# Two layers of 128x128 products on one core: each product given as two halves of 64 columns

## The chip, the cores and the metric

The kernel runs on one core of one Trainium2 chip. The metric is the device time of one execution in microseconds (us). Engines are named as the profile names them: PE is TensorE's matmuls, PEld its weight loads, DVE is VectorE, ACT is ScalarE, POOL is GpSimd, SP is SyncE, which issues DMAs.

## What is computed

The reference is an attention with a threshold, followed by a feed-forward layer with a squared ReLU, all in float32:

```
scores = scale * np.matmul(q, k.transpose(0, 1, 3, 2))       # q, k, v: (8, 8, 576, 64)
thresh = np.max(scores, axis=-1, keepdims=True) - tau
scores = np.where(scores >= thresh, scores, -1000000000.0)
attn = softmax(scores)
x = (attn @ v).transpose(0, 2, 1, 3).reshape(4608, 512)
h = np.maximum(x @ w_in, 0.0)                                # w_in:  (512, 2048)
out = h * h @ w_out                                          # w_out: (2048, 512)
```

The change touches the last two lines only: the two layers, x by w_in and h * h by w_out.

## The kernel before, in words

The kernel has three parts in order of time. **Attention** comes first: scores (L458), their softmax on DVE and ACT, transposes of the weights (L402, L422), spread sums (L541) and the product with v (L558). The array of TensorE is used there in tiles: L458, L541 and L558 have 64 rows and 64 columns, and the transposes 64 rows and 128 columns. A run of L558 (`values`) goes over nine blocks of keys c, two column halves u and two row halves j, so that its neighbouring calls lie on four different tiles of the array; the two u of one j share the rows and write to the same PSUM bank, into its lower and upper 64 partitions.

**The hidden layer** (`hidden_layer`, from 493.6 to 883 us) goes over 9 steps of 512 tokens each. Both layers multiply blocks by a scheme with 7 products in place of 8, applied twice, an outer index m and an inner index k of seven each, so a step has 49 block products. Sums and differences of the blocks are made on DVE, ACT and POOL before and after the products. The steps are run in passes (L1278 to L1279): step 0 alone, then steps 1 to 6 in pairs, each pair twice with one half h of the output columns, then steps 7 and 8 alone. A block product of a single step is four calls j on L984, each with 128x128 weights and 128 columns of x. A product of a pair of steps is two calls on L977, each with 128x128 weights and 256 columns.

**The output layer** (`output_layer`, from 883 us to the end) goes over the 9 steps, with 49 block products each. A product is four calls on L1119 which add up in PSUM: weights g[:, j, :] (the squared hidden values, 128x128), and 128 columns of w_out.

The order of a block row is written out in `inner` (L759): seven products with k = 1, 6, 7, 5, 2, 4, 3, each followed by its copy (L794, ACT) or sum (L125, DVE) out of PSUM, and by a `tick`, which issues other work: loads and sums for what comes next (`also`, L1295 and L1329), and the ReLU and square of finished tiles (`square`, L944). Products 1, 6, 7 and 5 begin new banks (X, Y, Z, W); products 2, 4 and 3 add to X, Z and W after the first sum has been read from them. Six banks are used in turn. Work on each engine is in program order. Weights stay in the tile `wall`: the 49 blocks of w_in first, which are replaced by those of w_out (L1207) in the last hidden step and at the start of the output layer.

[...] All matmuls are float32, for which the trace has two records of a call (two passes, each with its own weight load); a transpose has one.

Of the kernel before, what the change touches and what calls it, by code (L numbers as in the profile page):

```python
# [48 lines left out]
def kernel(  # L49
# [25 lines left out]
    nc = tc.nc  # L75
    B, H, S, D = q.shape
    P = 128
# [46 lines left out]
    def plus(e, out, x, y):  # L124
        e.tensor_tensor(out=out, in0=x, in1=y, op=ALU.add)  # L125
# [12 lines left out]
    W_IN, W_OUT = {}, {}  # L138
# [146 lines left out]
    HALF = P // 2  # L285
# [226 lines left out]
    for g in range(2, 2 * len(pairs)):  # L512
        two, x = divmod(g - 4, 4)
# [279 lines left out]
    def copy(to, from_):  # L793
        nc.scalar.copy(to, from_)  # L794

    NQ = STEP // 4


# [4 lines left out]
    def load_x(n, parts=XPARTS, slot=None):  # L803
        at = X_AT[n % 2]
        xo = arena[:, ds(at, 7 * BANK)].rearrange("p (m c t) -> p m c t", m=7, c=2)
        for a, c in parts:
            to = xo[:, AT_B[a][c] - 1, :, :] if slot is None else slot

            t0 = n * STEP + c * 2 * NQ
            done = 0  # L810
            while done < 2 * NQ:
                b, at = divmod(t0 + done, S)
                m = min(S - at, 2 * NQ - done)
                src = xT[b][ds(a * 2 * P, 2 * P), ds(at, m)].rearrange("(c p) n -> p c n", p=P)
# [21 lines left out]
    def prepare_x(n, add):  # L836
# [3 lines left out]
        for op, o, x, y in SUMS_B:  # L840
# [5 lines left out]
        of = {  # L846
            1: xo[:, :, 0, 0:NQ], 7: xo[:, :, 0, NQ : 2 * NQ], 2: xo[:, :, 1, 0:NQ], 3: xo[:, :, 1, NQ : 2 * NQ],
            5: xi[:, 0, :, :], 6: xi[:, 1, :, :], 4: xi[:, 2, :, :],
# [14 lines left out]
    def part_x(steps, k, m, count=None):  # L863

        of = slice((steps[0] + 1) % 2, (steps[0] + 1) % 2 + len(steps))
        ms = slice(m - 1, m - 1 + count) if count else m - 1
        if k in (1, 7, 2, 3):
            return places_x[:, of, ms, k in (2, 3), k in (7, 3), :]
        return sums_x[:, of, (5, 6, 4).index(k), ms, :]

    def slot_x(n, m):

        at = X_AT[n % 2]
        if m is None:
            return arena[:, ds(at + 7 * BANK, 3 * 7 * P)].rearrange("p (k z) -> p k z", k=3)[:, 0:2, 0:NQ * 2]
        return arena[:, ds(at + (m - 1) * BANK, BANK)].rearrange("p (c t) -> p c t", c=2)
# [64 lines left out]
    def hidden_bank():  # L941
        return banks.tile([P, BANK], FP32, tag="b", bufs=6, name="ph")
# [15 lines left out]
    def squares_due(wait):  # L958

        if squares and squares[0][0] + wait <= clock["n"]:  # L960
            square(*squares.popleft()[1:])

    def hidden_layer(n, also):

        steps, h = n
        of = prepared.pop(steps[0], None)
        tile4 = lambda tag, bufs: hid.tile([P, 4, NQ], FP32, tag=tag, bufs=bufs)
        bank = lambda: hidden_bank()[:, :].rearrange("p (k t) -> p k t", k=4)
        temp = lambda name: tile4("t", 6)
        U2, U3 = {}, {}  # L970

        for m in OUTER:

            def product(to, k, more):
                if h is not None:
                    for j in range(2):
                        nc.tensor.matmul(  # L977
                            to[:, 2 * j : 2 * j + 2, :], W_IN[m, k][:, ts(2 * h + j, P)], part_x(steps, k, m),
                            start=(not more and j == 0), stop=True, skip_group_check=True,
                        )  # L980
                    return
                x = of[k][:, m - 1, :] if of else part_x(steps, k, m)[:, 0, :]
                for j in range(4):
                    nc.tensor.matmul(  # L984
                        to[:, j, :], W_IN[m, k][:, ts(j, P)], x, start=(not more and j == 0), stop=True,
                        skip_group_check=True,
                    )

            def add(to, c, other, more, t=None):

                if other is None:
                    plus(nc.vector, to, c, more)
                else:
                    plus(nc.gpsimd, to, t, more)

            def final(ab, c, other):
                if m == 1:
                    U2[ab] = tile4("u", 12)
                    if other is None:
                        nc.scalar.copy(U2[ab], c)  # L1000
                    else:
                        plus(nc.vector, U2[ab], c, other)
                    return
                t = None
                if other is not None:
                    t = temp("t")
                    plus(nc.vector, t, c, other)
                if m == 6:
                    add(U2[ab], c, other, U2[ab], t)
                elif m == 7:  # L1010
                    U3[ab] = tile4("u", 12)
                    add(U3[ab], c, other, U2[ab], t)
                else:
                    o = tile4("o", 8)
                    add(o, c, other, U3[ab] if m in (4, 5) else U2[ab], t)
                    if m == 5:
                        add(U2[ab], c, other, U2[ab], t)
                    row, col = {2: (0, 0), 4: (1, 0), 5: (1, 1), 3: (0, 1)}[m]
                    squares.append((clock["n"] + LATER.get(m, 0), n, 4 * (2 * row + ab[0]) + 2 * col + ab[1], o))

            def tick(at):
                clock["n"] += 1
                also(m, at)
                squares_due(6)

            inner(product, copy, temp, bank, final, tick)


# [61 lines left out]
    def output_layer(n, also):  # L1090
        bank = lambda: banks.tile([P, BANK], FP32, tag="b", bufs=6, name="po")[:, 0:P]
        temp = lambda name: fin.tile([P, P], FP32, tag="t")
        AT = {(0, 0): 0, (1, 1): 1, (1, 0): 2, (0, 1): 3}
        U2 = fin.tile([P, 4, P], FP32, tag="u")
        U3 = fin.tile([P, 4, P], FP32, tag="u")
        o = {}

        def give_out(row, ab, queue):

            a, b = ab  # L1100
            to = out[ds(n * STEP + row * 2 * NQ + a * NQ, NQ), :].rearrange("p (c b o) -> p c b o", c=2, b=2)
            if queue is None:
                later.append((to[:, :, b, :], o[row][:, :, AT[ab], :]))
            else:
                queue.dma_start(out=to[:, :, b, :], in_=o[row][:, :, AT[ab], :])

        for m in OUTER:
            where = {2: (0, 0), 4: (1, 0), 5: (1, 1), 3: (0, 1)}.get(m)
            if where and where[0] not in o:
                o[where[0]] = fin.tile([P, 2, 4, P], FP32, tag="o")  # L1110
            mine = U3 if m in (4, 5) else U2
            t3 = fin.tile([P, 3, P], FP32, tag="t3") if m != 1 else None

            at_end = n == NSTEP - 1 and m == OUTER[-1]

            def product(to, k, more):
                g, w = operands[n, m, k], W_OUT[m, k].rearrange("p (k o) -> p k o", k=4)
                for j in range(4):
                    nc.tensor.matmul(  # L1119
                        to, g[:, j, :], w[:, j, :], start=(not more and j == 0), stop=(j == 3), skip_group_check=True  # L1120
                    )

            def sums_to(i, e, c):

                if where:
                    plus(e, o[where[0]][:, where[1], i, :], c, mine[:, i, :])
                if m in (5, 6):
                    plus(e, U2[:, i, :], c, U2[:, i, :])
                if m == 7:
                    plus(e, U3[:, i, :], c, U2[:, i, :])  # L1130

            def final(ab, c, other):
                i = AT[ab]
                if m == 1 and other is None:
                    nc.scalar.copy(U2[:, i, :], c)
                elif m == 1:
                    plus(nc.vector, U2[:, i, :], c, other)
                elif other is None:
                    sums_to(i, nc.vector, c)
                else:  # L1140
                    plus(nc.vector, t3[:, i - 1, :], c, other)
                    if at_end:
                        sums_to(i, nc.vector, t3[:, i - 1, :])
                if at_end:
                    give_out(0, ab, nc.sync if i % 2 else nc.scalar)

            inner(product, copy, temp, bank, final, lambda at: also(m, at))
            if m != 1 and not at_end:
                sums_to(slice(1, 4), nc.gpsimd, t3[:, :, :])
            if m in (5, 3) and not at_end:  # L1150
                for ab in AT:
                    give_out(where[0], ab, None)
# [8 lines left out]
    with tc.manual_schedule():  # L1161
# [149 lines left out]
        for n in range(NSTEP):  # L1311
            more = n + 1 < NSTEP
# [74 lines left out]
```

## Time and profile before

| what | value |
|---|---|
| median of 3 runs | 1287.91 us (1287.0 to 1290.93) |
| the profiled execution | 1285.38 us, of which the span of its instructions is 1283.3 us |
| attention | 0 to about 493 us |
| hidden layer, step 0 (L984) | from 493.6 us |
| hidden layer, steps 1 to 6 (L977) | from 537.4 us |
| hidden layer, steps 7 and 8 (L984) | about 795 to 883.4 us |
| output layer (L1119) | from 883.4 us; its last matmul starts at 1279.4 us |
| mean granted clock of TensorE | 0.996 |

How to read the lines: a group of instructions is given as source line, engine, operation, output<-inputs, the part of the array for TensorE (rows*columns), the shape of the moving data (or of the weights, for a load) and xcount; then the time in which at least one of them ran, the mean length of one in ns, and after the second bar the idle time of the engine before them and what ended it. Lengths of matmuls overlap their neighbours', so that they say little of the rate; counts in a stretch of time do. An answer for a window A:B counts each record that is in flight in it at any moment.

### The profile page before, as it was taken

The page shows a single profiled execution, that of the slowest core. Times are in us where ns is not written, and L with a number is a line of the kernel's source. Part 1 is how long each engine was busy: PE and PEld are TensorE (multiplying, and loading weights), DVE is VectorE, ACT ScalarE, POOL GpSimd, SP SyncE. Part 2 cuts the span into 40 slices and gives each one's busy share as a digit, 9 for nine tenths or more (in the row PEclk, how much of TensorE's full clock was granted, in tenths as well). Part 3 has the DMA queues.
Part 4 walks back from the last instruction along what each step waited for, and adds up shares of the span by engine and source line. Part 5 has one row for each costly group of instructions (what it writes and reads, how often), then busy time and mean ns, then how long its engine had stood idle before and what let it go on. Part 6 is the DMA issues. An engine that isn't in the chain of part 4 may idle for free.

```text
span 1283.3 us, 45875 instructions
## 1 busy us (share of the span) xinstructions
PE 1261.6 (98%) x18287; PEld 1105.9 (86%) x18287; DVE 989.2 (77%) x2384; ACT 846.2 (66%) x1537; POOL 981.5 (76%) x1070
## 2 busy tenths in 40 slices
PE   8999999999999999999999999999999999999998
PEld 5777777777777778988888888999999999999998
DVE  6999999999999994886877878867745664665463
ACT  6999999999999993665766766666423431343240
POOL 2999999777776543987997989758777867786775
PEclk8999999999999999999999999999999999999999
DMA  7566676444333314658767868499544314532411
GB/s 185 141 171 159 170 194 179 115 96 106 91 81 88 95 35 110 200 159 231 214 179 217 228 191 235 149 333 387 182 134 165 116 61 155 165 98 73 160 34 34
DMA packets 291413, 196.20 MB, mean 153 GB/s; under 512 B 100096, under 2 KB 252160, under 8 KB 291200
## 3 DMA queue, kind: packets, MB, share of 16 engines
q1 hardware_dynamic: 289888, 192.87, 51.7%
q8 instruction: 144, 2.36, 0.8%
q14 instruction: 69, 0.57, 0.1%
q10 hardware_dynamic: 1312, 0.41, 0.1%
HBM read 120.85 MB, written 72.35 MB: 151 GB/s over the span
## 4 chain that ended last, share of the span: by engine, by line
PE 75%; DMA 2%; ACT 2%; DVE 1%; issue 1%; SPq 0%; POOL 0%; DVEq 0%; ACTq 0%; POOLq 0%
PE po L1119 29%; PE ph L977 17%; PE ph L984 9%; PE sc L558 7%; PE sc L458 6%; PE pt L402 4%; PE sc L541 1%; PE sc L422 1%; DMA wall<-w 1%; DMA g<-arena 1%; DVE arena L125 1%; ACT arena L946 1%; ACT arena L947 1%; ACT c L833 0%; DMA arena<-xT 0%
## 5 line engine op out<-in xcount | busy, mean ns | idle before, releaser
L125 POOL TENSOR_TENSOR arena<-arena 128x512 f32<-128x512 f32 (+1 forms) x314 | 378.1, 1222 | 135.1 <-DVE arena L125 117.2
L1119 PE MATMUL po<-wall,arena 128*128 128x128 f32 x3528 | 394.8, 275 | 1.4 <-ACT arena L794 1.4
L1119 PEld LDWEIGHTS po<-wall,arena 128*128 128x128 f32 x3528 | 394.3, 192 | 1.8 <-ACT arena L794 1.8
L125 DVE TENSOR_TENSOR arena<-ph,arena 128x512 f32<-128x512 f32 x378 | 255.2, 689 | 78.8 <-PE ph L977 30.3
L122 POOL TENSOR_TENSOR arena<-arena 128x128 f32<-128x128 f32 (+1 forms) x322 | 265.3, 825 | 26.1 <-DMA arena<-w 10.3
L977 PE MATMUL ph<-arena,wall 128*128 128x256 f32 x1176 | 256.3, 380 | 2.1 <-DVE arena L125 1.7
L977 PEld LDWEIGHTS ph<-arena,wall 128*128 128x128 f32 x1176 | 222.1, 190 | 35.9 <-DVE arena L125 6.0
L125 DVE TENSOR_TENSOR arena<-po,arena 128x128 f32<-128x128 f32 x378 | 108.3, 290 | 167.8 <-PE po L1119 163.7
L491 DVE SCALAR_TENSOR_TENSOR arena<-arena 128x576 f32<-128x576 f32 x288 | 226.1, 821 | 0.6 <-ACT arena L486 0.6
L486 ACT ACTIVATE arena<-arena 128x576 f32<-128x576 f32 x288 | 213.8, 780 | 13.1 <-DVE arena L476 13.1
L833 ACT COPY c<-arena 128x512 f32<-128x512 f32 (+1 forms) x295 | 169.1, 579 | 72.7 <-DVE arena L122 35.7
L476 DVE TENSOR_SCALAR_CACHE_REDUCE arena<-sc 128x576 f32<-128x576 f32 x288 | 203.3, 753 | 13.8 <-issue 5.2
L458 PE MATMUL sc<-arena 64*64 64x512 f32 (+1 forms) x2304 | 178.1, 413 | 5.8 <-ACT arena L549 1.7
L558 PE MATMUL sc<-arena 64*64 64x128 f32 (+1 forms) x5760 | 166.0, 262 | 0.8 <-ACT arena L549 0.7
L122 DVE TENSOR_TENSOR arena<-arena,c 128x512 f32<-128x512 f32 x235 | 154.4, 666 | 11.9 <-ACT c L833 8.9
L558 PEld LDWEIGHTS sc<-arena 64*64 64x64 f32 x5760 | 151.3, 134 | 3.9 <-ACT arena L549 0.9
L549 ACT COPY arena<-pt 128x1024 f32<-128x1024 f32 x144 | 145.9, 1013 | 4.3 <-PE pt L402 3.7
L794 ACT COPY arena<-po 128x128 f32<-128x128 f32 x63 | 16.7, 265 | 186.4 <-PE po L1119 183.6
L458 PEld LDWEIGHTS sc<-arena 64*64 64x64 f32 x2304 | 76.4, 134 | 70.7 <-issue 45.7
L984 PE MATMUL ph<-arena,wall 128*128 128x128 f32 x1176 | 132.0, 275 | 0.6 <-DVE arena L691 0.6
L984 PEld LDWEIGHTS ph<-arena,wall 128*128 128x128 f32 x1176 | 131.6, 192 | 0.9 <-issue 0.7
L483 POOL TENSOR_SCALAR arena<-arena,tau_p 128x2 f32<-128x2 f32 x144 | 83.3, 579 | 54.0 <-DVE arena L476 41.0
(54 smaller groups left out, 1142.2 us busy)
## 6 DMA issues: line engine op xcount, KB each, us to landing
arena<-g SPq DMA_DIRECT2D x144, 256.0 KB, 4.8
g<-arena SPq DMA_DIRECT2D x192, 128.0 KB, 2.8
w<-arena SPq DMA_DIRECT2D x60, 256.0 KB, 3.1
wall<-w SPq DMA_DIRECT2D x49, 256.0 KB, 5.2
g<-arena SPq DMA_DIRECT2D x48, 256.0 KB, 3.6
arena<-w SPq DMA_DIRECT2D x44, 256.0 KB, 3.2
arena<-in_v_dram SPq DMA_DIRECT2D x32, 288.0 KB, 3.9
out_dram<-arena SPq DMA_DIRECT2D x70, 128.0 KB, 2.2
```

The costliest lines, as they stand in the source:

```text
L122: e.tensor_tensor(out=out, in0=x, in1=y, op=ALU.subtract)
L125: e.tensor_tensor(out=out, in0=x, in1=y, op=ALU.add)
L458: made = nc.tensor.matmul(sc[at, ds(to, count)], lhs, kT[rows, ds(at_k, count)], start=True, stop=True)
L476: made = nc.vector.tensor_scalar(out=s[:, j, :], in0=sc[:, ds(at, S)], scalar1=1.0, scalar2=None, op0=ALU.mult, op1=ALU.min, accum_out=nmx ...
L486: nc.scalar.activation(out=w[:, :, j, :], in_=of(j), func=AF.Exp, bias=nmx[:, j : j + 1], scale=-1.0)
L491: nc.vector.scalar_tensor_tensor(out=w[:, :, j, :], in0=of(j), scalar=thr[:, j : j + 1], in1=w[:, :, j, :], op0=ALU.is_le, op1=ALU.mult, a ...
L549: touch("weights", nc.scalar.copy(joined(to), whole(pt, 0, count)), at, 2 * BANK, m)
L558: made = nc.tensor.matmul(sc[ds(u * D, D), ds(5 * j * BANK + row, count)], loaded_v[i][rows, (c - (u != j)) % CH, :], wT[m][rows, ds(weigh ...
L833: nc.scalar.copy(c, y)
L977: nc.tensor.matmul(to[:, 2 * j : 2 * j + 2, :], W_IN[m, k][:, ts(2 * h + j, P)], part_x(steps, k, m), start=(not more and j == 0), stop=Tr ...
L984: nc.tensor.matmul(to[:, j, :], W_IN[m, k][:, ts(j, P)], x, start=(not more and j == 0), stop=True, skip_group_check=True,)
L1119: nc.tensor.matmul(to, g[:, j, :], w[:, j, :], start=(not more and j == 0), stop=(j == 3), skip_group_check=True)
```

## The change

A helper `by_tiles` takes the place of `nc.tensor.matmul` at two places. It gives one product as two matmuls: the left 64 columns of the weights into partitions 0 to 63 of the output, then the right 64 columns into partitions 64 to 127. Both have all 128 rows, and both read the same moving data. HALF is 64. The calls with 256 columns (L977) stay as they are.

```
+    def by_tiles(to, lhs, rhs, start, stop):
+
+        for cols in (ds(0, HALF), ds(HALF, HALF)):
+            nc.tensor.matmul(to[cols], lhs[:, cols], rhs, start=start, stop=stop, skip_group_check=True)
...
                 for j in range(4):
-                    nc.tensor.matmul(
-                        to[:, j, :], W_IN[m, k][:, ts(j, P)], x, start=(not more and j == 0), stop=True,
-                        skip_group_check=True,
-                    )
+                    by_tiles(to[:, j, :], W_IN[m, k][:, ts(j, P)], x, not more and j == 0, True)
...
                 for j in range(4):
-                    nc.tensor.matmul(
-                        to, g[:, j, :], w[:, j, :], start=(not more and j == 0), stop=(j == 3), skip_group_check=True
-                    )
+                    by_tiles(to, g[:, j, :], w[:, j, :], not more and j == 0, j == 3)
```

## The prediction

> **What bounds the kernel now.** I read the page's first two parts, then the groups by line with the shapes kept apart, then the stages in windows. The page:
>
> ```profile
> span 1283.3 us, 45875 instructions
> PE 1261.6 (98%) x18287; PEld 1105.9 (86%) x18287; DVE 989.2 (77%) x2384; ACT 846.2 (66%) x1537; POOL 981.5 (76%) x1070
> ...
> PEclk8999999999999999999999999999999999999999
> ...
> PE 75%; DMA 2%; ACT 2%; DVE 1%; issue 1%; SPq 0%; POOL 0%; DVEq 0%; ACTq 0%; POOLq 0%
> ```
>
> TensorE is busy nearly throughout at the full granted clock, and it heads the chain that ended last. Busy alone does not say what a matmul waits for, since matmuls are pipelined; the spacing of their starts does. The groups, matmuls (PE) and their weight loads (PEld):
>
> ```profile
> L1119 PE MATMUL po<-wall,arena 128*128 128x128 f32 x3528 | 394.8, 275 | 1.4 <-ACT arena L794 1.4
> L977 PE MATMUL ph<-arena,wall 128*128 128x256 f32 x1176 | 256.3, 380 | 2.1 <-DVE arena L125 1.7
> L558 PE MATMUL sc<-arena 64*64 64x128 f32 x4608 | 164.0, 273 | 0.8 <-ACT arena L549 0.7
> L984 PE MATMUL ph<-arena,wall 128*128 128x128 f32 x1176 | 132.0, 275 | 0.6 <-DVE arena L691 0.6
> ```
>
> ```profile
> L1119 PEld LDWEIGHTS po<-wall,arena 128*128 128x128 f32 x3528 | 394.3, 192 | 1.8 <-ACT arena L794 1.8
> L558 PEld LDWEIGHTS sc<-arena 64*64 64x64 f32 x5760 | 151.3, 134 | 3.9 <-ACT arena L549 0.9 <-DVE arena L476 0.3
> L402 PEld LDWEIGHTS pt<-ident,arena 64*128 64x128 f32 x2304 | 83.7, 140 | 42.4 <-ACT arena L549 32.7 <-issue 4.6 <-ACT arena L427 1.1
> ```
>
> The code makes 9 x 49 x 4 = 1764 calls on L1119, and the trace has 3528 records: each call is two passes, and each pass loads its own weights. L984 likewise (3 steps, 588 calls, 1176 records). The change touches these two groups and not L977, whose calls have 256 columns. Three windows without a stall, one inside each group (columns: PE, PEld, DVE, ACT, POOL with record counts, clock, DMA share, GB/s):
>
> ```profile
> 640.00:680.00 40.00, 40.00 (x187) 35.20 (x187) 30.61 (x49) 24.98 (x46) 34.89 (x44) 1.00 0.67 183
> 1000.00:1040.00 40.00, 40.00 (x361) 40.00 (x360) 23.59 (x61) 14.21 (x29) 30.89 (x27) 1.00 0.43 133
> 810.00:850.00 40.00, 40.00 (x361) 40.00 (x360) 29.74 (x48) 25.77 (x48) 27.70 (x28) 1.00 0.57 193
> ```
>
> A window counts every record that touches it, so the spacing is (window + length of one record) / count. L1119 (1000:1040) and L984 (810:850): (40.00 + 0.275) / 361 = 111.57 ns a pass. L977 (640:680): (40.00 + 0.379) / 187 = 215.9 ns for 256 columns, so 107.9 ns per 128. So streaming alone does not account for 111.57 ns. The loads do: with 256 columns PEld has gaps (35.20 of 40), with 128 columns it is busy all 40.00. I read L1119 and L984 as **bound by the weight load**, by some 2 to 4 ns a pass, with the stream close behind.
>
> **What the change does to one pass.** It takes away 1764 + 588 calls of 128 x 128 weights and gives twice as many with 64 columns of weights: 4704 passes become 4704 pairs of passes, a left and a right half, each streaming the same 128 columns. All hangs on whether the two halves of a pair run side by side. Before has no tile of 128 rows x 64 columns; the nearest are the 64 x 64 tiles of L558, four on the array, two side by side on the same rows. Two answers in the middle of one run of them, the first for 302.646:302.647, the second for 302.646:303.846:
>
> ```profile
> L558 PE MATMUL sc<-arena 64*64 64x128 f32 x10 | 0.5, 269 | 0.0
> L558 PE MATMUL sc<-arena 64*64 64x128 f32 x54 | 1.7, 269 | 0.0
> ```
>
> 44 more records in 1.200 us are 27.27 ns each, **109.1 ns for four**. With 128 columns each, these four cannot have run one after another (one stream is 107.9): all four tiles stream at once, neighbours on the same rows too, and writing the same bank. And four such tiles take 2.5 ns less than one pass of the whole array. The load explains it: a record of 64 columns lasts 134 ns, one of 128 columns 192 ns.
>
> Are loads shorter because of fewer columns, or fewer rows? In ordinary matmuls of before both change together. Transposes part them, as they load 128 columns from 64 rows (L402, 140 ns) and, at the start (the load in flight at 6.75 us), from 128 rows:
>
> ```profile
> L1171 PEld LDWEIGHTS sc<-ident 128*128 128x128 f32 x1 | 0.1, 141 | 0.0
> ```
>
> Twice the rows, 140 and 141 ns: rows cost nothing, in this kind of load. I take it that they cost nothing in the other kind, and that a half's load is that of L558. [...]
>
> Can two halves on the same rows load fast enough? A pair needs two loads in 109 ns, 54.6 ns each. In runs of L558 that mix 64 and 128 columns, at 114.0:114.001 and 114.0:115.167, loads first, then the 64-column matmuls:
>
> ```profile
> L558 PEld LDWEIGHTS sc<-arena 64*64 64x64 f32 x9 | 0.3, 133 | 0.0
> L558 PEld LDWEIGHTS sc<-arena 64*64 64x64 f32 x69 | 1.4, 134 | 0.0
> ```
>
> ```profile
> L558 PE MATMUL sc<-arena 64*64 64x64 f32 x8 | 0.4, 218 | 0.0
> L558 PE MATMUL sc<-arena 64*64 64x64 f32 x48 | 1.6, 218 | 0.0
> ```
>
> 60 loads in 1.167 us on two row halves are 30 for each, one per 38.9 ns: faster than needed. The 64-column matmuls run on two of the four tiles, 20 on each, one per 58.4 ns; as half of 107.9 is 54, that spacing is again about a load's. So a load of 58 ns recurred every 39 ns on the same rows: neighbours load side by side.
>
> Issue: a pair asks for one matmul per 54.6 ns; L558 was fed one per 27.27, and the whole attention ran 12092 records in 480 us, one per 39.7:
>
> ```profile
> 0.00:480.00 480.00, 468.44 (x12092) 348.45 (x12096) 458.17 (x1316) 450.43 (x791) 357.46 (x440) 0.99 0.50 127
> ...
> 883.00:1283.00 400.00, 395.22 (x3534) 394.65 (x3532) 224.89 (x584) 136.70 (x283) 299.26 (x252) 1.00 0.38 125
> ```
>
> So issue costs nothing. Bounds for a pair: from below 107.9 ns (the stream), from above 2 x 109.1 = 218.2 ns (the halves in turn). I take **109.1**, L558's, the nearest row.
>
> **The sum.** 4704 x (111.57 - 109.1) = 11.6 us gained, 8.7 of it in the output layer. What of that is given back:
>
> ```profile
> PE po L1119 <- ACT arena L794: 1.4, 2, 0.9
> ...
> PEld ph L977 <- DVE arena L125: 6.0, 12, 2.1
> ```
>
> ```profile
> 900.62 0.63 ACT arena L947
> 901.25 0.16 ACT arena L794
> 901.45 10.65 PE po L1119 x93
> ```
>
> Up to 901.45 the output layer's start (18 us) is paced by ACT, which still squares the first layer's last tiles ahead of the copy that TensorE waits for: 2.2% of 18 us, 0.4 us, turns into longer waits. The first step's pass (392 pairs, 1.0 us gained) is followed by L977's waits for DVE; I leave half, 0.5 us, as lost. After 902 nothing else comes close: the window 883:1283 has POOL at 299 and DVE at 225 of 400 us, and TensorE waited on L1119 only the times shown. Should a sum by POOL come late after all, at most these 8.3 us (8.7 - 0.4) are at stake. Changes of tile shape: whole passes and the whole output layer are of one shape, so two more changes come (into and out of the 256-column passes). In attention such changes leave no gap between records (start, length):
>
> ```profile
> 301.30 0.71 PE L402 MATMUL pt<-ident,arena 64*128 64x64 f32 x16
> 301.94 2.24 PE L558 MATMUL sc<-arena 64*64 64x128 f32 x69
> ```
>
> Nothing at best, one drained record (0.27 us) each at worst; I take 0.3 for both. No wait is added: the pieces of a product stand together on TensorE's queue with the same semaphores, no DMA moves, and the reader waits for the last right half. Net 11.6 - 0.4 - 0.5 - 0.3 = **10.4 us**. The profiled execution took 1285.4 us (span 1283.3 and 2.1 around it), so 1275.0; the median of the runs is 2.5 us above it, so against 1287.91 I forecast **1277.5 us**.
>
> **Rivals.**
>
> *The halves in turn (slower).* If two column halves with all 128 rows cannot stream at once, a pair takes 218.2 ns: 4704 x 106.6 = +501 us, 1789 us. For it: every side-by-side pair in this trace is on 64 rows, and none shows 128. Against: L558's neighbours share rows and bank and do overlap. It is slower as soon as a pair takes more than 111.57 ns. 9%.
>
> *Loads no longer hidden (slower).* If a half's load must wait until the other half's stream on the same rows is through, 58.4 ns come bare: 109.1 + 58.4 = 167.5 ns, 4704 x 55.9 = +263 us, 1551 us. Against: L1119's loads already lie beside a matmul on the same rows, or 275 ns and 192 ns records would not alternate every 111.57 ns. [...] 8%.
>
> *No change.* If the two halves' loads go one after another after all, or rows do count, a pair stays at the old 111.57 ns, as two loads of 64 columns in a row are one of 128: 1288 us. Against: the 38.9 ns and the 140 against 141 ns above. That the change doesn't do what it says, one half being run on the whole array's shape, is the first rival's price. 8%.
>
> **How the numbers follow.** Forecast 75%; its own range is 1272 (the stream's own 107.9 ns, 17.3 us gained, 1.2 given back: 1271.8) to 1283 (half of the gain lost). The range: with no change added, up to the highest run shown, about 1292, it holds 83%; the two slower cases lie far off and are left out. A measurement of this kernel tells about 0.3%, 3.9 us, from no change; the forecast lies beyond it, so faster 0.75, same 0.08, slower 0.17.
>
> **What would show it.** L1119 and L984 as 128*64 with 7056 and 2352 records; in the window 1000:1040 about (40 + 0.27) / 0.0546 = 738 matmul records (721 if nothing changed, 370 in turn); load records near 134 ns; L977 still at 215.9 ns. Wrong if the halves' starts lie 109 ns apart instead of closer, if loads stay at 192 ns, or if waits of L1119 for DVE or POOL rise above 3 us.

## The result, and the profile after

The changed kernel takes **1281.49 us** (median of 6 runs, 1279.87 to 1282.9) against 1288.26 us before (median of 6): ratio **0.9947**, 95% interval 0.9930 to 0.9964. That is 6.8 us faster, 4.6 to 9.0 by the interval; the forecast was 10.4. The profiled execution took 1281.21 us, with a span of 1279.1 us.

The first lines of the page of the changed kernel (all matmuls of both halves now stand on L799, the helper's line):

```profile
span 1279.1 us, 55422 instructions
PE 1252.5 (98%) x22991; PEld 1093.8 (86%) x22991; DVE 987.5 (77%) x2384; ACT 845.6 (66%) x1537; POOL 982.4 (77%) x1070
```

The groups of the output layer (po) and of the hidden layer's single steps (ph), matmuls and loads:

```profile
L799 PE MATMUL po<-wall,arena 128*64 128x128 f32 x7056 | 388.3, 273 | 4.2 <-ACT arena L794 2.8 <-DVE arena L125 0.6 <-issue 0.4
...
L799 PE MATMUL ph<-arena,wall 128*64 128x128 f32 x2352 | 129.2, 273 | 0.6 <-DVE arena L691 0.6
```

```profile
L799 PEld LDWEIGHTS po<-wall,arena 128*64 128x64 f32 x7056 | 386.7, 137 | 5.6 <-ACT arena L794 3.8 <-DVE arena L125 1.2 <-issue 0.6
```

The shape is 128*64 with twice the records, and a load lasts 137 ns in place of 192. The same three windows as before:

```profile
640.00:680.00 40.00, 40.00 (x187) 35.21 (x186) 30.67 (x50) 25.59 (x47) 35.41 (x45) 1.00 0.68 188
1000.00:1040.00 40.00, 40.00 (x738) 40.00 (x736) 24.01 (x62) 15.00 (x31) 31.12 (x27) 1.00 0.41 134
810.00:850.00 40.00, 40.00 (x738) 40.00 (x736) 30.73 (x49) 26.28 (x49) 28.54 (x29) 1.00 0.57 191
```

738 records in 40 us: (40.00 + 0.273) / 738 = 54.57 ns for one half, **109.1 ns for a pair**, where one whole pass took 111.57. The count is the one forecast. The 256-column passes (640:680) kept their 187 records.

So away from any stall the change does what the sum says. Where is the rest? The first and last start of each group, in us after the min/median/max length (changed kernel):

```profile
L799 PE MATMUL po<-wall,arena x7056: 272/273/421, 883.0 to 1275.2; 128*64 128x128 f32 x196
L799 PE MATMUL ph<-arena,wall x2352: 272/273/323, 495.9 to 882.9; 128*64 128x128 f32 x196
L982 PE MATMUL ph<-arena,wall x1176: 379/379/483, 538.8 to 796.7; 128*128 128x256 f32 x196
```

and of the kernel before:

```profile
L1119 PE MATMUL po<-wall,arena x3528: 275/275/377, 883.4 to 1279.4; 128*128 128x128 f32 x196
...
L977 PE MATMUL ph<-arena,wall x1176: 379/379/483, 537.4 to 795.4; 128*128 128x256 f32 x196
```

| stage | before | after | difference | sum in the prediction |
|---|---|---|---|---|
| attention, up to the first hidden matmul | 493.6 | 495.9 | +2.3 | 0 |
| step 0 (to the first 256-column pass) | 43.8 | 42.9 | -0.9 | -1.0 |
| 256-column passes, first to last start | 258.0 | 257.9 | -0.1 | 0 |
| steps 7 and 8 (to the first output matmul) | 88.0 | 86.3 | -1.7 | -1.9 |
| output layer, first to last start | 396.0 | 392.2 | **-3.8** | **-8.7** |

Both single-step stages gave nearly all that 109.1 ns promise. The output layer gave less than half. Waits of TensorE and of the engines that feed it, between 880 and 935 us of the changed kernel (total, times, longest, in us):

```profile
POOL arena L125 <- DVE arena L125: 10.7, 6, 3.8
...
ACT arena L794 <- POOL arena L125: 4.8, 1, 4.8
...
PEld po L799 <- ACT arena L794: 3.8, 3, 3.0
ACT c L838 <- DMA arena<-g: 3.6, 1, 3.6
...
DVE arena L125 <- DMA g<-arena: 3.0, 1, 3.0
...
PEld po L799 <- DVE arena L125: 1.2, 2, 0.9
```

Read it from the bottom up: DVE waits 3.0 us for the store of a squared tile (g<-arena), whose buffer it needs; POOL waits for DVE, ACT's copy for POOL, and TensorE's loads 3.0 us for the copy. The same answer for the kernel before has a shorter wait of the copy, 1.1 us as the longest for TensorE, and no wait for a store:

```profile
ACT arena L794 <- POOL arena L125: 2.8, 1, 2.8
...
PEld po L1119 <- ACT arena L794: 1.8, 2, 1.1
```

Two windows of the changed kernel show what comes of it (columns as above):

```profile
886.60:889.40 2.80, 0.09 (x2) 0.00 (x0) 0.53 (x1) 0.22 (x2) 2.73 (x3) 1.00 1.00 353
890.20:893.20 3.00, 3.00 (x32) 3.00 (x30) 2.04 (x5) 2.14 (x5) 2.73 (x3) 0.50 1.07 400
```

In the first TensorE stands still, with the DMA engines full (share 1.00). In the second it works at **half the granted clock**: a pair takes 214 ns ((3.00 + 0.42) / 32 = 107 ns for one half, taking 0.42 us, the longest record above). The 3 us at half clock cost another 1.5 us at least. The profile of before has none at this place, nor while the matmuls of its output layer run; it has one late in attention, from 484.5 to 487.7 us, behind a wait of 1.8 us.

### The profile page after: what moved, and what is told of

It reads as the page before. It is cut to its first block, busy times and chain, and to the rows that moved or that the text cites. A ratio compares the mean times of both kernels' runs of the same rounds, so it can differ in the third digit from the quotient of the medians.

```text
span 1279.1 us, 55422 instructions
## 1 busy us (share of the span) xinstructions
PE 1252.5 (98%) x22991; PEld 1093.8 (86%) x22991; DVE 987.5 (77%) x2384; ACT 845.6 (66%) x1537; POOL 982.4 (77%) x1070
## 4 chain that ended last, share of the span: by engine, by line
PE 74%; DMA 2%; DVE 2%; ACT 1%; issue 1%; SPq 0%; POOL 0%; DVEq 0%; POOLq 0%; ACTq 0%
PE po L799 27%; PE ph L982 18%; PE ph L799 10%; PE sc L558 7%; PE sc L458 6%; PE pt L402 4%; PE sc L541 1%; PE sc L422 1%; DVE arena L125 1%; DMA arena<-g 1%; ACT c L838 1%; PE sc L402 0%; DMA wall<-w 0%; DVE arena L122 0%; ACT arena L951 0%
## 5 line engine op out<-in xcount | busy, mean ns | idle before, releaser
L799 PE MATMUL po<-wall,arena 128*64 128x128 f32 x7056 | 388.3, 273 | 4.2 <-ACT arena L794 2.8
L799 PEld LDWEIGHTS po<-wall,arena 128*64 128x64 f32 x7056 | 386.7, 137 | 5.6 <-ACT arena L794 3.8
L982 PEld LDWEIGHTS ph<-arena,wall 128*128 128x128 f32 x1176 | 222.1, 190 | 36.0 <-DVE arena L125 5.8
L558 PE MATMUL sc<-arena 64*64 64x128 f32 (+1 forms) x5760 | 165.9, 261 | 1.3 <-ACT arena L549 0.8
L558 PEld LDWEIGHTS sc<-arena 64*64 64x64 f32 x5760 | 150.7, 133 | 4.9 <-issue 1.0
L799 PE MATMUL ph<-arena,wall 128*64 128x128 f32 x2352 | 129.2, 273 | 0.6 <-DVE arena L691 0.6
L799 PEld LDWEIGHTS ph<-arena,wall 128*64 128x64 f32 x2352 | 128.3, 137 | 1.4 <-issue 1.0
```

The lines of the kernel that those rows point to most:

```text
L558: made = nc.tensor.matmul(sc[ds(u * D, D), ds(5 * j * BANK + row, count)], loaded_v[i][rows, (c - (u != j)) % CH, :], wT[m][rows, ds(weigh ...
L799: nc.tensor.matmul(to[cols], lhs[:, cols], rhs, start=start, stop=stop, skip_group_check=True)
L982: nc.tensor.matmul(to[:, 2 * j : 2 * j + 2, :], W_IN[m, k][:, ts(2 * h + j, P)], part_x(steps, k, m), start=(not more and j == 0), stop=Tr ...
```

## The experiments

The theory at their start: a pass of 128 columns waits for its weight load; two halves load and stream side by side, 109.1 ns; and what is missing is lost at the hand-over from the hidden to the output layer, which TensorE now reaches sooner while the DMAs there (reloads of the weight tile, stores of squared tiles) come no sooner. The rivals: a fixed cost of a whole-array pass in place of the load; a chance stall of one execution; engines' own work at the hand-over.

### again: the changed kernel once more

> The changed kernel once more, to see which parts of its profile recur. In the first profile a pair of halves came every 109.1 ns, so 4704 pairs should have given 11.6 us; the stage of the output layer gave only 3.8 of its 8.7 us, with a stall of TensorE of 3.1 us at its start (886 us) and a stretch of half the clock behind it. Theory (the gain is lost at the hand-over between the layers, where the stores of the squared tiles stand behind weight reloads on SP's queue): again about 0.995 of before, pairs every 109.1 ns, and again 3 to 6 us of stalls between 885 and 935 us, of varying length and place. Rival (a chance stall of that one execution): stalls as before, about 2 us, and a ratio of 0.991.

Measured: 1279.87 us, ratio 0.9940 (0.9924 to 0.9957). Its first and last start, its waits from 880 to 935, and two windows:

```profile
L799 PE MATMUL po<-wall,arena x7056: 272/273/422, 882.0 to 1272.8; 128*64 128x128 f32 x196
```

```profile
PEld po L799 <- ACT arena L794: 2.6, 2, 2.3
DVE arena L125 <- DMA g<-arena: 2.2, 1, 2.2
...
PEld po L799 <- DVE arena L125: 0.8, 1, 0.8
```

```profile
885.60:887.60 2.00, 0.04 (x2) 0.00 (x0) 0.00 (x0) 0.26 (x2) 2.00 (x3) 1.00 0.97 345
888.70:891.90 3.20, 3.20 (x34) 3.20 (x32) 2.19 (x5) 3.04 (x7) 2.48 (x2) 0.50 1.06 400
```

The same stall at the same place, for the same store, followed by the same half clock: not the chance of one execution, though its length varies, as wide_too shows below. The output layer took 390.8 us. Without any stall it would be 3527 pairs x 109.1 = 384.8, so 6.0 us are lost here and 7.4 in the first profile. Before, 3527 x 111.57 = 393.5 stand against 396.0, so 2.5 are lost. The extra loss is **3.5 to 4.9 us** in these two profiles.

### mov64: the loads doubled instead

The kernel before, with the moving data of the output layer split and not the weights:

```
 for j in range(4):
+    for i in range(2):
         nc.tensor.matmul(
-            to, g[:, j, :], w[:, j, :], start=(not more and j == 0), ...
+            to[:, ts(i, HALF)], g[:, j, :], w[:, j, ts(i, HALF)], start=(not more and j == 0 and i == 0), ...
```

> From the kernel before: each product of the output layer is given as two with the whole 128x128 weights and the left or right 64 columns of the moving data, so every load comes twice and the streams are halved. Theory (a pass of 128 columns waits for its weight load, 111.6 ns): each half pass still takes 111.6 ns, so the output layer takes 2 x 394 us and the kernel about 1288 + 393 = 1680 us. [...]

Measured: 1676.72 us. The matmuls, and the window 1000:1040:

```profile
L1120 PE MATMUL po<-wall,arena 128*128 128x64 f32 x7056 | 788.0, 275 | 0.0
```

```profile
1000.00:1040.00 40.00, 40.00 (x361) 40.00 (x360) 11.47 (x29) 6.84 (x14) 15.15 (x13) 1.00 0.00 1
```

361 records in 40 us, just as with 128 columns: a pass of 64 columns takes the same 111.57 ns as one of 128, so the stream does not set it; the loads, the same in both, leave no gap (40.00 of 40). The fixed-cost rival is out: with half of L977's 215.9 ns as the stream, the fixed part would be 3.6 ns, a pass of 64 columns would take 57.6 ns and the kernel some 1301 us (an estimate from these spacings). The kernel ran once in this form; theory and rival are some 380 us apart.

### out_only and hid_only: one layer alone

The edits undo one of the two replacements each (the four-call loop of the other layer is as before).

> Only the output layer's products are given as halves; the hidden layer is as before. Theory: TensorE reaches the output layer no earlier than before, so SP's queue is as far along as before; 3528 x 2.47 = 8.7 us less some 1 to 4 us of stalls at the layer's start: ratio 0.994 to 0.996, hidden layer unchanged in its windows. Rival (the output layer gains less because each half costs something in its place): no more than 3.8 us, ratio 0.997, with stalls of about 2 us as before.

> Only the hidden layer's products of single steps are given as halves (1176 pairs); the output layer is as before. Theory: 1176 x 2.47 = 2.9 us gained up to the end of the hidden layer, then lost in part at the hand-over: ratio 0.998 to 1.000. Rival (nothing is lost there): 0.9977.

Measured: out_only 1278.81 us, ratio 0.9933 (0.9913 to 0.9952); hid_only 1284.71 us, 0.9978 (0.9962 to 0.9995). The output layer of out_only, then of hid_only:

```profile
L799 PE MATMUL po<-wall,arena x7056: 272/273/324, 890.6 to 1278.8; 128*64 128x128 f32 x196
```

```profile
L1121 PE MATMUL po<-wall,arena x3528: 275/275/377, 878.2 to 1275.0; 128*128 128x128 f32 x196
```

The theory of out_only holds and its rival (0.997) is out. out_only takes 388.2 us there, 3.4 above 384.8: it loses only 0.9 us more than before, with 1.2 us as the longest wait for ACT's copy, and gets 7.8 of the 8.7 us. hid_only takes 396.8, 0.8 longer than before, though its output layer is the old one. Where the hidden steps are in halves, DVE waits for a store; where they are whole, it doesn't. The wait stands in hid_only too (window 857:928, as its hand-over comes at 878 us), and out_only has none:

```profile
DVE arena L125 <- DMA g<-arena: 1.7, 1, 1.7
```

So the two halves of the change work against each other: with the last hidden steps shortened, DVE needs a buffer before its store is through. Of the 2.6 us (0.9 + 1.7) by which the hand-over comes sooner, only the 1.7 of steps 7 and 8 can matter for that, as the transfers of the last step move with the rest. As times of the whole kernel, the intervals of the changed kernel and of out_only overlap; which is better is not told. hid_only's 0.9978 is the rival's number (nothing lost), but its interval holds the theory's as well.

### wide_too: the 256-column products in halves as well

```
-                        nc.tensor.matmul(to[:, 2 * j : 2 * j + 2, :], W_IN[m, k][:, ts(2 * h + j, P)], ...)
+                        by_tiles(to[:, 2 * j : 2 * j + 2, :], W_IN[m, k][:, ts(2 * h + j, P)], ...)
```

> The changed kernel, and the 256-column products of the hidden layer are given as halves too. [...] Rival (a half pass is cheaper by a fixed 2.5 ns on any tile of 64 columns): 1176 x 2.5 = 2.9 us less, 255 us, ratio 0.992.

Measured: 1279.37 us, ratio 0.9960 (0.9940 to 0.9980). The window 640:680:

```profile
640.00:680.00 40.00, 40.00 (x375) 26.41 (x370) 30.86 (x50) 26.53 (x49) 35.30 (x45) 1.00 0.67 186
```

(40.00 + 0.380) / 375 = 107.7 ns a half, 215.4 a pair, against 215.9 for a whole pass; one record more or less in the count is 0.6 ns a pair. The loads became shorter (PEld busy 26.41 of 40 in place of 35.20) and it gains no more than that, as they were hidden already. So the change takes away a wait for loads, and where there was none the ratio stayed (0.9960 against 0.9947). The rival's 2.5 ns a pass are out.

The run tells something of the hand-over as well, as its last hidden steps and its output layer are those of the changed kernel. DVE waits only 1.0 us for the store here, TensorE at most 1.2 us, and no half clock follows. The output layer takes 389.1 us (884.3 to 1273.4): 4.3 lost, 1.8 more than before.

### quarters: four tiles of 32 columns

```
-        for cols in (ds(0, HALF), ds(HALF, HALF)):
+        for cols in [ts(i, P // 4) for i in range(4)]:
```

> The changed kernel with four quarters of 32 columns in place of two halves. Theory (with halves the stream of 128 columns is the bound, and tiles of a row of the array run side by side however many): four quarters every 109.1 ns, ratio 0.994 as with halves. [...]

Measured: 1370.27 us, ratio **1.0657** (1.0637 to 1.0677). Matmuls and loads of the output layer, and two answers in one run of them, for 1032.5:1032.501 and 1032.5:1033.156:

```profile
L799 PE MATMUL po<-wall,arena 128*32 128x128 f32 x14112 | 406.8, 273 | 37.8 <-issue 35.6
```

```profile
L799 PEld LDWEIGHTS po<-wall,arena 128*32 128x32 f32 x14112 | 383.7, 110 | 60.7 <-issue 59.1 <-DVE arena L125 0.4
```

```profile
L799 PE MATMUL po<-wall,arena 128*32 128x128 f32 x10 | 0.5, 273 | 0.0
L799 PE MATMUL po<-wall,arena 128*32 128x128 f32 x34 | 1.1, 273 | 0.0
```

While it runs, 24 more records in 0.656 us are 27.3 ns each and 109.3 for four: quarters go no lower than the 109.1 of halves, so this part of the theory holds. But TensorE now idles with "issue" as the reason (a wait for nothing that the profile shows), which the profile of before never had in this layer. In all, (406.8 + 37.8) us / 14112 = 31.5 ns a record, slower than the 27.3 that it asks for. Halves ask for one record per 54.6 ns. The rival that issue becomes the bound, and that the layers grow by whatever lies above 109.1 ns, is right in its number: four records take 126 ns. The pauses have a pattern (start, length, then the pause before it):

```profile
927.76 3.69 PE L799 MATMUL po<-wall,arena 128*32 128x128 f32 x126 [0.51 <-issue]
931.68 3.69 PE L799 MATMUL po<-wall,arena 128*32 128x128 f32 x126 [0.22 <-issue]
```

From 927 to 1003 us each stretch between two pauses has 126 to 128 records, or twice or five times 126. The queue that fetches instructions (q8 on the page) moved 255 packets, against 144 before: 14112 more matmuls and as many loads are 254 to a packet, 127 of each (the changed kernel, with 9408 records and 37 packets more than before, has 254 as well). So the pauses come where a new packet of instructions is due. That the fetching is what holds TensorE is a reading of these counts; no run was made for it.

### store_act and before_store_act: the stores on another queue

```
+            queue = nc.scalar if steps[0] == NSTEP - 1 else nc.sync
-            nc.sync.dma_start(out=gT[steps[0]][j]...
+            queue.dma_start(out=gT[steps[0]][j]...
```

> The changed kernel; the stores of the squared tiles of the last hidden step are issued by ACT in place of SP, so that they no longer stand behind the weight reloads on SP's queue. Theory (TensorE stalls at the hand-over because DVE waits for a buffer whose store stands behind reloads): the 2.3 to 3.1 us stall at 885 us and the half clock behind it go, 3 to 5 us of stalls become 1 to 3, ratio 0.990 to 0.992. Rival (the DMA engines are full there, and the order of issue does not matter): stalls of 5 to 7 us stay, ratio 0.994.

> The kernel before with the same move of the last hidden step's stores to ACT's queue. Theory: before had 2.1 us of stalls at the hand-over, so at most 1 to 2 us are gained: ratio 0.998 to 1.000, and the change is worth more on top of it (about 0.992 between the two) than without. Rival (the order of issue does not matter): 1.000, and the change is worth 0.994 on it as before.

Measured: store_act 1289.41 us, 1.0026 (1.0010 to 1.0042); before_store_act 1293.47 us, 1.0061 (1.0045 to 1.0077). Both are slower than the kernel before. SP's queue and a window of store_act, and TensorE's waits for the copy between 880 and 935 us:

```profile
872.38 20.40 SPq L1208 DMA_DIRECT2D wall<-w  x23
```

```profile
872.00:893.00 21.00, 17.32 (x280) 16.20 (x276) 10.70 (x17) 12.10 (x20) 13.23 (x12) 0.92 1.04 378
```

```profile
PEld po L799 <- ACT arena L794: 5.9, 3, 3.4
```

SP's own waits in that window, and two of ACT's between 880 and 935 us:

```profile
SPq L1208 <- DMA wall<-w: 9.7, 19, 1.0
```

```profile
ACT c L838 <- DMA wall<-w: 1.9, 1, 1.9
...
ACT arena L794 <- DMA g<-arena: 1.2, 1, 1.2
```

With no store in between, SP still needs 20.4 us for 23 reloads, and for 9.7 us of it waits for earlier reloads: the DMA engines are full (1.04 share). DVE no longer waits for a store, but ACT does the waiting now, and everything behind it. My picture of a store stuck behind reloads on **SP's queue** is not borne out: taking the stores off that queue gains nothing and makes the waits longer. How much of a store's delay is its place in the queue and how much its transfer, the edit doesn't tell. Both theories missed, and the rivals too, which had 0.994 and 1.000. The gain of the change on top of it is 1.0026 / 1.0061 = 0.9965.

### noreload: the reloads taken away

```
         t = weight_tile(W_OUT, m, k)
-        nc.sync.dma_start(out=t[:, :], in_=w_dram[ds(at * P, P), :])
```

> The kernel before without the 49 reloads of the weight tile at the end of the hidden layer and the start of the output layer; it leaves them out, so the output layer multiplies by what lies in the tile. Theory (the last hidden step and the hand-over are held by DMAs: 39 reloads, 16 loads and 16 stores of 256 KB in 43 us are 18.6 MB, 430 GB/s, where the busiest slice of the profile moved 387): the 2.1 us of stalls go, output layer about 394 us, ratio 0.998. Rival (stalls there are ACT's and DVE's own work): 1.000.

> The changed kernel without the 49 reloads, which it leaves out too. Theory: with the DMAs gone the hand-over gives nothing back: output layer 385.5 us, hidden layer as in the changed kernel, 11.6 us (0.991) between this run and the kernel before without reloads, 0.989 to the kernel before. Rival (the loss is in the engines' work at the hand-over, reached too early): stalls of 3 to 7 us stay and 0.994 to 0.995 between the two.

Both kernels multiply by what lies in the tile. Measured: noreload_before 1287.03 us, 0.9999 (0.9986 to 1.0012); noreload_after 1281.11 us, 0.9953 (0.9937 to 0.9969). The window 864:890, before and then noreload_after:

```profile
864.00:890.00 26.00, 25.43 (x228) 25.24 (x227) 18.20 (x31) 14.37 (x27) 23.95 (x20) 1.00 1.05 391
```

```profile
864.00:890.00 26.00, 25.23 (x464) 24.99 (x460) 18.80 (x30) 13.16 (x24) 23.13 (x19) 1.00 0.23 83
```

The output layers, noreload_before and noreload_after, and the latter's waits from 880 to 935:

```profile
L1119 PE MATMUL po<-wall,arena x3528: 275/275/377, 886.1 to 1282.2; 128*128 128x128 f32 x196
```

```profile
L799 PE MATMUL po<-wall,arena x7056: 272/273/324, 885.2 to 1273.9; 128*64 128x128 f32 x196
```

```profile
ACT arena L794 <- POOL arena L125: 2.8, 1, 2.8
ACT c L838 <- DMA arena<-g: 2.7, 1, 2.7
...
PEld po L799 <- ACT arena L794: 2.2, 2, 1.2
...
PEld po L799 <- DVE arena L125: 0.8, 1, 0.8
```

With the DMA engines at a quarter of their load, the wait for a store is gone, the stall is 1.2 us, and no half clock follows (its longest matmul record there is 324 ns, against 421 and 422 where it does): the output layer takes 388.7 us, 3.9 lost. noreload_before takes 396.1 as before, so the 2.5 us lost there do not come from the reloads. The profiles side by side (waits in us; lost is the output layer less 384.8 us for halves, 393.5 for whole passes):

| run | last hidden steps | output layer | reloads | DVE's wait for the store | longest wait for the copy | half clock behind it | lost |
|---|---|---|---|---|---|---|---|
| before | whole | whole | yes | none | 1.1 | no | 2.5 |
| noreload_before | whole | whole | no | none | 1.0 | no | 2.6 |
| out_only | whole | halves | yes | none | 1.2 | no | 3.4 |
| noreload_after | halves | halves | no | none | 1.2 | no | 3.9 |
| hid_only | halves | whole | yes | 1.7 | 1.5 | no | 3.3 |
| wide_too | halves | halves | yes | 1.0 | 1.2 | no | 4.3 |
| again | halves | halves | yes | 2.2 | 2.3 | yes | 6.0 |
| the changed kernel | halves | halves | yes | 3.0 | 3.0 | yes | 7.4 |

The store is waited for where the hidden steps are in halves and the reloads run, in four profiles of four, and in no other row. How long the wait is differs between these profiles, and only its two longest stalled TensorE for more than 1.5 us. So in three profiles of the same layer, with 1.8 to 4.9 us of extra loss, **0.4 to 3.5 come with the full DMA engines** (4.3, 6.0 or 7.4 less 3.9) and **about 1.4 stay without them** (0.9 in out_only). The second part has a place of its own: TensorE waits 0.8 us for DVE, which sums the next step's blocks behind ACT's copies, and those wait for the blocks' loads (arena<-g); the kernel before had no wait of L1119 for DVE. By the stalls each side was partly right. By the kernels' times the theory (0.991 between the two) missed and the rival's 0.994 to 0.995 came: 0.9953 against 0.9999 is no better than 0.9947. So the profiles show the loss at the hand-over, and the times do not show that it goes with the reloads. In the profile noreload_after spent 2.2 us more than its partner in the 256-column passes (261.2 against 259.0), which the change does not touch: TensorE waited 2.3 us for DVE once there, and its longest record took 773 ns, against 483 in the partner.

### slow: the reloads spread

In both kernels 26 in place of 39 reloads are issued in the last hidden step, and 23 in place of 10 in the output layer:

```
-                if 7 * i + at > 9:
-                    reload(7 * i + at - 10)
+                if 7 * i + at > 9 and (7 * i + at) % 3:
+                    reload(slow.index(7 * i + at))
...
-                if n == 0 and 7 * i + at < 10:
-                    reload(39 + 7 * i + at)
+                if n == 0 and 3 <= 7 * i + at < 15:
+                    for r in range(26 + 2 * (7 * i + at - 3), min(49, 28 + 2 * (7 * i + at - 3))):
+                        reload(r)
```

> The kernel before with the reloads spread: 26 in place of 39 in the last hidden step, two of three ticks, and the other 23 early in the output layer, two to a tick from the fourth. Nothing is left out. Theory: fewer DMAs beside the last stores, at most 1 to 2 us less: ratio 0.998 to 1.000. Rival: the late reloads arrive too late, and TensorE waits for them: above 1.001.

> The changed kernel with the reloads spread in the same way; a version that might beat both. Theory: the stall at 885 us and the half clock behind it go, stalls fall from 5.6 to 7.0 us to 1 to 3: ratio 0.990 to 0.992. Rival: the late reloads hold TensorE up, or other transfers do, and the ratio stays 0.994 or above.

Measured: slow_before 1295.06 us, 1.0067 (1.0047 to 1.0086); slow_after 1284.46 us, 0.9983 (0.9968 to 0.9997). The waits of slow_after from 880 to 935:

```profile
ACT c L838 <- DMA arena<-g: 7.5, 1, 7.5
...
PEld po L799 <- ACT arena L794: 3.9, 3, 1.6
```

The 3 us wait is gone (longest now 1.6), and so is the wait for the store, but the loads of the next step's g come behind the reloads: TensorE waits 2.3 us for DVE, has half the clock from 925 to 930 us (0.50), and the output layer takes 393.8 us (886.7 to 1280.5), more than in the changed kernel. The rival was right: other transfers hold TensorE up. In slow_before it is the same, with 8.7 us as the wait for the g loads and 3.2 us as TensorE's for DVE; there the rival's number came, but not by waits for the reloads themselves. None of these versions is shown to beat the changed kernel.

## Why the prediction was right, and where it was not

- **The bound.** "Bound by the weight load, by some 2 to 4 ns a pass": right. mov64 shows it best: half the columns, the same 111.57 ns.
- **109.1 ns a pair.** Right to the digit (738 records in the window, forecast 738). The nearest row, four tiles of L558, was the right one, though it had 64 rows and not 128; that the third digit agrees as well is more than that row could promise.
- **Rows cost nothing in a load.** Right within 3 ns: a load of 64 columns lasts 134 ns with 64 rows (L558) and 137 with 128 (L799). With all 128 rows it is 192, 137 and 110 ns for 128, 64 and 32 columns, some 27 for every 32.
- **Issue costs nothing.** Right for halves, for a reason weaker than I gave. One record per 27.27 ns in L558 is a burst of 72; quarters, which need that rate without end, got 31.5 ns. The row that carries the step is the whole attention's 39.7 ns. Halves have a trace of the same pauses: TensorE waits 0.4 us for "issue" once in the output layer, and none before.
- **The rivals.** Halves in turn (1789) and bare loads (1551) did not happen. In the changed kernel the halves have all rows, and their loads run beside the streams: both engines are busy for 40.00 of 40 us, at 109.1 ns a pair with load records of 137 ns. What lets a load run beside a matmul on the same rows, no run here shows. "No change" is out by the interval.
- **What is given back** is the term that was too small, 1.2 us in all, and with it the time: 10.4 us forecast, 6.8 measured, which the forecast's own range (half of the gain lost, 1283 us) still holds. I booked 0.4 us at the start of the output layer, 0.5 in step 0 and 0.3 for changes of shape. Step 0 gave back 0.1, steps 7 and 8 some 0.2, all of which the changes of shape may be. The output layer gave back 4.9 in the changed kernel's profile, 3.5 and 1.8 in two others of the same layer. "2.2% of 18 us" took the wait there as paced by ACT alone. I had read which engine TensorE waits for, and not what that engine's chain waits for when it is reached sooner: a store into full DMA engines (1.05 share over 864:890 in the profile of before already, though no store was waited for there). A stall of 2.3 or 3.0 us then also cost clock. "After 902 nothing else comes close" was wrong as well, by the wait for the g loads that ended at 918 us and those of TensorE up to 931 us (0.4 us for "issue", 1.2 for DVE). These waits for DVE stayed below the 3 us that the prediction gave as a sign of being wrong.
- **The bounds.** The highest run shown before was 1290.9 us; the prediction wrote about 1292 for it. "Full granted clock nearly throughout" read a row with one digit per 32 us, in which 3 us of half clock leave a 9.
- **What stays open.** Attention took 2.3 us longer in the changed kernel's profile, with the same code; the prediction had put it at nothing. Over all 14 profiles the first hidden matmul starts between 491.7 and 498.6 us; the eight whose output layer has its weights split average 2.8 us later than the six others. Part of it is there by 40 us: in the changed kernel's profile, again and out_only TensorE has 541 to 545 matmul records by then, in before, mov64 and hid_only 625 to 629. In the changed kernel's profile TensorE stood 1.6 us for a load of q, up to 28.2 us, and had a granted clock of 0.50 from 30 to 33 us, where before had 1.00. Why is not settled, and no run was made for it. So the 6.8 us of the medians, and the 8.6 of the second measurement (again, 1288.46 less 1279.87), hold the layers' gain (6.5 us in the one profile) and differences of this kind, which I cannot tell apart.

## What to carry to other kernels

Look at the spacing of the matmuls, not at their busy time: here it stayed at 111.57 ns with half the moving columns (mov64) and PEld had no gap (40.00 of 40), so the weight load was the bound, and splitting the weights by columns hid it, down to 109.1 ns and no further (107.9 is half of L977's spacing; quarters got 109.3). The output layer's gain on TensorE arrived where its feeders were not paced by something else (7.8 of 8.7 us in out_only), and less where they were (3.8 in the changed kernel); before booking such a gain, look at the DMA share in the window ahead of each hand-over, and at what the feeders wait for. The stalls of 2.3 and 3.0 us were paid twice here, the second time in clock (0.50 for some 3 us).

## What was not expected of the hardware

- After waits of 2.3 and 3.0 us TensorE's granted clock was 0.50 for 3 us and more (890.20:893.20 and 888.70:891.90 above), although it was working again; the 1.2 us stall of noreload_after at the same place was followed by none. Shorter ones were followed by it too: in attention TensorE stood still for 1.7 us before 484.4 us (before) and 1.6 us before 28.2 us (the changed kernel), with half the clock for some 3 us soon after (0.50 over 484.5 to 487.7 and 30 to 33 us).
- Four tiles of 128 rows x 32 columns run side by side at 109.3 ns, but over a whole layer TensorE ran only one float32 matmul record with its load per 31.5 ns, with pauses after every 126 to 128 records.
- With the DMA engines full (1.04 share), issues of 256 KB on SP came 20.40 / 23 = 0.89 us apart, with 9.7 of the 20.40 us spent waiting for earlier ones; on ACT such waits held ACT's own work up (1.9 us before a copy).
